# w_in loaded by contraction tile, w_out transposed on TensorE, some early loads on ScalarE's queue

## The chip, the cores and the metric

The kernel runs on one core of one Trainium2 chip. The metric is the device time of one execution in microseconds (us). The kernel before takes 674.87 us, the median of 3 runs (673.68 to 677.32).

## The reference

Three parts follow each other: a linear attention with decay over 768 steps (4 batches, 8 heads of 48), a dense layer with `g = h * cos(h)`, and a layer that sends each token to one of eight experts, or to none.

```python
# r, k, v: (4, 8, 768, 48); state starts at 0
for t in range(S):
    cur = einsum('bhd,bhe->bhde', u[None] * kt, vt)
    y[:, :, t] = einsum('bhd,bhde->bhe', rt, state + cur)
    state = w[None, :, :, None] * state + einsum('bhd,bhe->bhde', kt, vt)
x = y.transpose(0, 2, 1, 3).reshape(3072, 384)

h = x @ w_in                      # (384, 2048)
x = (h * cos(h)) @ w_out          # (2048, 384)

do_compute = x @ w_skip > 0
e_idx = argmax(x @ w_gate, axis=1)          # 8 experts
out = x                                     # where do_compute is False
out = x + gate * (relu(x @ w1[e]) @ w2[e])  # elsewhere, e of the token
```

## The kernel before

Tokens go through in 12 chunks of 256 (64 steps of each batch). For each chunk c the attention loads two tiles of r and k (`rk`, step ldr) and two of r, k, v in natural order (`nat`, step ldn), scales them on VectorE and GpSimd (km, rm, knm, pr1, pr2, cc, am), and multiplies on TensorE: A (r with k), Y (with v), Yz (with the carried state), U (the new state). The result goes into `xt` as a high and a low float16 part (xh on ScalarE, xl on VectorE), and six small transfers (xx) put 16-partition pieces in their place.

The dense layer takes the chunk as group g. G1(g, f), f = 0 to 7, multiplies `xt` by `w_in`: 18 matmuls of 256 columns into one PSUM tile, then the chain cn (ScalarE), cr (VectorE), cs (ScalarE, sine), cg (VectorE), ch (ScalarE), cl (VectorE or GpSimd) gives g in two float16 parts. G2(g, t, q), t = 0 and 1, q = 0 to 3, multiplies by w_out: 12 matmuls a quarter.

All weights are split into a high and a low part as well. The inputs w_in and w_out are 8-byte words. A piece is loaded (step ld), VectorE makes float32 of it in three passes (wu L448, wx L454, wv L460), ScalarE writes the high part (wh), VectorE or GpSimd the low one (wl). w_in comes in 8 pieces of 256 columns of all three contraction tiles, so each row gives a run of 2 KB; w_out in 8 pieces of two rows of 3 KB for each partition.

The 9 scores of the last part (skip and gate) are linear in the dense layer's output, so w_out times `w_skip` and `w_gate` gives 9 more columns of w_out (DM to NO, 384 to 393). For each of 16 tiles k of w_out two DMA transposes (wt, L508) bring its high and low part into `wt`, nine matmuls (wm) multiply it by a float16 pair of the 27 score weights (`sgh`), and at the end wph and wpl write the high and low part of all 16. The very first G2 does without these columns, and a step of its own, G2(0, 0, l), adds them later, with 48 matmuls of 9 columns.

After the twelfth group the tokens of each expert are gathered and go through the expert matmuls in 16 tiles; that part is not touched.

The order is not written by hand. Every step is added to a `Plan` with its engine, a cost, its dependences and a priority; a list scheduler in `Plan.order` sets the order on each engine from them. The table `SHIFT` moves priorities, the table `ENGINE` picks the engine of a step, and `PIECES` says in which order the pieces of w_in and w_out take their priorities. Engines then work in that order, each waiting for what its next instruction needs. The queue SP starts nearly all transfers; ScalarE (ACT) starts three at the beginning.

Of the kernel before, what the change touches and what calls it, by code (L numbers as in the profile page):

```python
# [40 lines left out]
SG = 2.0 ** 2  # L41
# [15 lines left out]
class Plan:  # L57
# [28 lines left out]
    def order(self):  # L86
# [15 lines left out]
        while any(ready.values()):  # L102
# [57 lines left out]
PIECES = "iioiiiooioioiooo"  # L160
PIECE_0, PIECE_STEP = -40, 8
SHIFT = {
# [18 lines left out]
    "sgl": 280, "tab0": 300, "tabi": -310, "tkd": -260, "tkn": -360, "tkt": 400, "vb_0_0": 50, "vb_1_1": 150,  # L181
# [13 lines left out]
):
    ENGINE.update(dict.fromkeys(_ks.split(), _e))


def group(key):
# [8 lines left out]
    if n in ("wt", "wm"):  # L208
        return f"{n}_{key[1] // 4}"
# [33 lines left out]
def _kernel(ctx, tc, rk, nat, wcol, small, ci, w_in, w_out, w1, w2, out):  # L243
# [56 lines left out]
    sgh = cp.tile([128, 2, 3, 9], F16, name="sgh")  # L300
# [43 lines left out]
    add("cst", "A", 2700, f, prio=-900, nbytes=400e3)  # L344

# [997 lines left out]
```

## Time and profile before

| | |
|---|---|
| median of 3 runs | 674.87 us |
| the profiled execution | 674.17 us |
| its span, first to last instruction | 672.4 us |
| mean granted TensorE clock | 0.961 |
| busy: TensorE, VectorE, ScalarE, GpSimd | 593.0, 423.4, 305.8, 300.8 us |
| DMA: moved, mean rate over the span | 87.04 MB, 129 GB/s |

The span is what the profile shows instruction by instruction; the execution's own time has 1.8 us more around it. PE is TensorE, PEld its weight loads, DVE VectorE, ACT ScalarE, POOL GpSimd, SP the sync engine, whose queue is SPq. TensorE's clock has two levels; the granted clock of a stretch is 1.00 if all of it ran at the upper one and 0.50 if all of it ran at the lower one. An engine's busy time in a stretch, and what ended its idle time, are read beside each other: an engine may be idle because it waits, or because it is done.

### The profile page before, as it was taken

The numbers are of one execution on the slowest core, as the hardware profiler recorded it, in microseconds if no ns is written. First come the engines' busy times: TensorE is split into PE (matmuls) and PEld (weight loads), VectorE is DVE, ScalarE is ACT, GpSimd is POOL, SyncE is SP. The second block draws the span as 40 slices with busy tenths as digits, with TensorE's granted clock in tenths as the row PEclk, the third lists the DMA queues.
The fourth block names the chain that finished last, engine by engine and source line by source line (L and its number), as shares of the span: only waits on it lengthen the run. The fifth ranks groups of instructions, "written<-read, shape, count | busy, mean of one in ns | idle before, by whom it ended". The sixth has DMA issues, their size and how long they took to land. (4 is left out here: it accounts for less than half of the span.)

```text
span 672.4 us, 17390 instructions
## 1 busy us (share of the span) xinstructions
PE 593.0 (88%) x7191; PEld 441.1 (66%) x7191; DVE 423.4 (63%) x828; ACT 305.8 (45%) x522; POOL 300.8 (45%) x269
## 2 busy tenths in 40 slices
PE   1325659699999999999999999999999989999993
PEld 1314438567768777777777777777776768777662
DVE  5877858856857654645564655454686568777650
ACT  2224536432536454444444454444674146555530
POOL 3342426456866575657464543233353152232111
PEclk9996759789999999999999999999999999999997
DMA  8979877567272215160504210010768238889820
GB/s 181 224 172 236 197 146 190 119 144 204 69 181 73 79 33 148 27 153 4 157 25 123 58 32 26 22 34 7 235 220 185 51 92 233 267 237 242 249 86 18
DMA packets 83075, 87.04 MB, mean 129 GB/s; under 512 B 35838, under 2 KB 70956, under 8 KB 82994
## 3 DMA queue, kind: packets, MB, share of 16 engines
q1 hardware_dynamic: 79746, 80.67, 47.9%
q0 software_dynamic: 2816, 4.91, 2.5%
q8 instruction: 57, 0.93, 0.6%
q10 hardware_dynamic: 432, 0.33, 0.2%
q14 instruction: 24, 0.20, 0.1%
HBM read 66.57 MB, written 13.73 MB: 119 GB/s over the span
## 5 line engine op out<-in xcount | busy, mean ns | idle before, releaser
L264 PE MATMUL ps_o<-wo,gt 128*128 128x393 f16 (+2 forms) x1200 | 211.1, 329 | 0.0
L264 PE MATMUL ps_h<-xt,wih 128*128 128x256 f16 x1152 | 200.6, 279 | 7.4 <-DVE s L741 7.4
L264 PEld LDWEIGHTS <-gt 128*128 128x128 f16 x1200 | 113.3, 99 | 76.3 <-issue 5.2
L264 PE MATMUL ps_h<-xt,wil 128*128 128x256 f16 x576 | 160.7, 279 | 0.0
L746 POOL TENSOR_TENSOR gt<-s,gt 128x512 f16<-128x512 f32 x87 | 105.1, 1214 | 107.1 <-ACT gt L274 106.7
L264 PEld LDWEIGHTS <-wih 128*128 128x128 f16 x1152 | 112.9, 100 | 29.8 <-DVE s L741 7.9
L734 DVE SCALAR_TENSOR_TENSOR s<-s,ps_h 128x512 f32<-128x512 int32 x96 | 65.4, 684 | 89.3 <-ACT s L730 89.2
L737 ACT ACTIVATE s<-s 128x512 f32<-128x512 f32 x96 | 60.0, 629 | 58.2 <-DVE s L734 58.2
L730 ACT ACTIVATE s<-ps_h 128x512 int32<-128x512 f32 x96 | 56.9, 592 | 59.4 <-PE ps_h L264 57.1
L274 ACT ACTIVATE gt<-s 128x512 f16<-128x512 f32 x87 | 54.4, 628 | 56.6 <-DVE s L741 56.6
L741 DVE SCALAR_TENSOR_TENSOR s<-s,ps_h 128x512 f32<-128x512 f32 x87 | 59.2, 683 | 33.4 <-ACT s L737 33.3
L264 PE MATMUL ps_h<-xe,w 128*128 128x256 f16 (+1 forms) x720 | 65.8, 251 | 2.9 <-issue 1.1
L264 PE MATMUL ps_o<-w,hh 128*128 128x384 f16 x384 | 64.9, 326 | 1.6 <-DVE hh L1112 1.4
L281 DVE SCALAR_TENSOR_TENSOR w<-ws,w 128x768 f16<-128x768 f32 (+1 forms) x56 | 60.0, 1084 | 8.8 <-ACT w L274 8.4
L264 PEld LDWEIGHTS <-w 128*128 128x128 f16 x720 | 58.8, 98 | 9.6 <-issue 2.3
L264 PEld LDWEIGHTS <-wil 128*128 128x128 f16 x576 | 57.8, 100 | 7.8
L274 ACT ACTIVATE w<-ws 128x768 f16<-128x768 f32 (+1 forms) x56 | 51.1, 928 | 16.8 <-DMA ws<-in_w_dram 14.0
L264 PEld LDWEIGHTS <-hh 128*128 128x128 f16 x384 | 36.9, 98 | 26.1 <-DVE hh L1112 2.5
L1141 POOL DMA_INDIRECT out_dram<-xg,recs x16 | 18.5, 1156 | 71.3 <-DVE xg L1136 54.8
L873 POOL DMA_INDIRECT tab<-rec,di x24 | 24.6, 1025 | 45.6 <-DVE osum L867 23.1
L552 POOL TENSOR_TENSOR k<-rk,tk 112x512 f32<-112x512 f32 x20 | 27.7, 1383 | 33.9 <-DMA rk<-in_rk_dram 26.3
L1107 ACT ACTIVATE hh<-ps_h 128x512 f16<-128x512 f32 (+1 forms) x40 | 20.2, 510 | 35.7 <-PE ps_h L264 31.4
(129 smaller groups left out, 614.8 us busy)
## 6 DMA issues: line engine op xcount, KB each, us to landing
nat<-in_nat_dram SPq DMA_DIRECT2D x96, 144.0 KB, 4.5
ws<-in_w_dram SPq DMA_DIRECT2D x24, 512.0 KB, 5.6
ws<-in_w_dram SPq DMA_DIRECT2D x32, 384.0 KB, 4.5
rk<-in_rk_dram SPq DMA_DIRECT2D x24, 448.0 KB, 5.5
so<-in_w_out_dram SPq DMA_DIRECT2D x8, 768.0 KB, 11.3
xd<-y SPq DMA_DIRECT2D x24, 192.0 KB, 2.0
out_dram<-y SPq DMA_DIRECT2D x48, 96.0 KB, 2.2
si<-in_w_in_dram SPq DMA_DIRECT2D x16, 192.0 KB, 5.8
```

The costliest lines, as they stand in the source:

```text
L264: return T.matmul(o, lhsT=l, rhs=r, start=start, stop=stop)
L274: return A.activation(out=o, in_=i, func=AF.Copy, scale=scale)
L281: V.scalar_tensor_tensor(out=o, in0=x, scalar=scale, in1=hi, op0=ALU.mult, op1=ALU.subtract)
L552: add((name, c, x), e, cost, lambda: ENG[e].tensor_tensor(out=o(), in0=a(), in1=b(), op=op), deps, pr)
L730: A.activation(out=n, in_=d["ph"], func=AF.Copy, scale=1.0 / (TWO_PI * SH), bias=0.25)
L734: V.scalar_tensor_tensor(out=d["s"], in0=d.pop("n"), scalar=-TWO_PI * SH, in1=d["ph"], op0=ALU.mult, op1=ALU.add)
L737: lambda: A.activation(out=d["s"], in_=d["s"], func=AF.Sin, scale=1.0 / SH, bias=math.pi / 2), [("cr", g, f)], pr)
L741: V.scalar_tensor_tensor(out=o, in0=s, scalar=0.5, in1=ph, op0=ALU.mult, op1=ALU.mult)
L746: lambda: ENG[e].tensor_tensor(out=gt[g][1][:, 2 * f:2 * f + 2], in0=d.pop("g"), in1=gt[g][0][:, 2 * f:2 * f + 2], op=ALU.subtract), [("ch ...
L873: P.indirect_dma_start(out=tab[:, :], out_offset=bass.IndirectOffsetOnAxis(ap=di[:, t], axis=0), in_=rec[:, t], in_offset=None, bounds_che ...
L1107: A.activation(out=d["hh"][:, 0, 2 * f_:2 * f_ + 2, 0:N], in_=d["ph", f_][:, :, 0:N], func=AF.Relu)
L1141: P.indirect_dma_start(out=out[:, :], out_offset=bass.IndirectOffsetOnAxis(ap=xo["recs"][:, s, 1:2], axis=0), in_=xs_.pop(s), in_offset=No ...
```

## The change

- **w_in** comes in 6 pieces instead of 8: one contraction tile of 128 rows and half of the columns each, so a row gives a run of 8 KB. A piece takes four transfers, to 48 and 16 partitions at a time. G1(g, f) now needs three pieces: all three contraction tiles of its half.
- **w_out** is transposed on TensorE: six matmuls with an identity add the high and the low part into PSUM (wt), ScalarE copies the float32 result (wc), three float32 matmuls multiply it by the scores' weights (wm), and ScalarE and VectorE write the high and low part of these 9 columns for each k (wph, wpl). The two PSUM tiles of G2 serve for it in turn. The first group's G2 has the 9 columns from the start, waits for all 16 wpl, and the step G2(0, 0, l) is gone.
- **Queues:** a load whose step stands in the new table row "A" of `ENGINE` is started by ScalarE.
- The tables `SHIFT`, `ENGINE` and `PIECES` have other numbers, so the order on every engine is another.

```diff
-PIECES = "iioiiiooioioiooo"
+PIECES = "ioiiioiioooooo"
...
+    ("A", """ld_i_0 ld_i_4 ld_o_0 ld_o_6 ld_o_7 ldn_0_1 ldn_1_0 ldn_3_0 ldn_3_1 ldr_2_1 ldr_3_1 xx_2"""),
...
+    def dq(eng):
+        return A if eng == "A" else nc.sync
...
-    def w_in_piece(f_, prio):
-        def src(t):
-            m = slice(256 * WW * f_, 256 * WW * (f_ + 1))
-            v = w_inv[0:288, m].rearrange("(j i p) n -> i p j n", j=3, i=2)
-            x = w_inv[288:384, m].rearrange("(i j p) n -> i p j n", i=2, j=3)
-            for i in range(2):
-                nc.sync.dma_start(out=t[64 * i:64 * i + 48, 0:3:2], in_=v[i, :, 0:3:2])
-                nc.sync.dma_start(out=t[64 * i:64 * i + 48, 1], in_=v[1 - i, :, 1])
-                nc.sync.dma_start(out=t[64 * i + 48:64 * i + 64], in_=x[1 - i])
+    def w_in_piece(i, prio):
+        j, m = i % 3, slice(F_ * (i // 3), F_ * (i // 3 + 1))
+        def src(t, q):
+            for x in range(2):
+                a, b = 96 * j + 48 * (x ^ (j % 2)), 288 + 48 * (1 - x) + 16 * j
+                v = w_inv[:, WW * m.start:WW * m.stop].unsqueeze(1)
+                q.dma_start(out=t[64 * x:64 * x + 48], in_=v[a:a + 48])
+                q.dma_start(out=t[64 * x + 48:64 * x + 64], in_=v[b:b + 16])
...
-            wt_[k] = wt = ap.tile([128, 2, 3, 128], F16, tag="wt", name="wt", bufs=2)
-            for i in range(2):
-                nc.sync.dma_start_transpose(out=wt[:, i], in_=wo[:, k, i, 0:DM])
-        add(("wt", k), "Q", 2400, f, [("wl", "o", k // 2), ("wm", k - 2)], wpr["o", k // 2] - 50, 100e3)
+            wt_["p", k] = p = pt("o", [128, 512], bufs=2)
+            for j in range(3):
+                for i in range(2):
+                    mm(p[:, 128 * j:128 * j + 128], wo[:, k, i, 128 * j:128 * j + 128], ident, i == 0, i == 1)
+        add(("wt", k), "PE", 330, f, [("wl", "o", k // 2), "cst16", ("wpl", k - 2)], wpr["o", k // 2] - 5)
...
+            wt_["t", k] = t = ap.tile([128, 3, 128], F32, tag="wt", name="wt", bufs=2)
+            copy(A, t.rearrange("p a b -> p (a b)"), wt_["p", k][:, 0:DM])
+        add(("wc", k), "A", c_a(DM, True), f, [("wt", k), ("wm", k - 2)], wpr["o", k // 2] - 5)
...
             for j in range(3):
-                mm(p, wt[:, 0, j], sgh[:, 0, j], j == 0, False)
-                mm(p, wt[:, 0, j], sgh[:, 1, j], False, False)
-                mm(p, wt[:, 1, j], sgh[:, 0, j], False, j == 2)
+                mm(wt_["p", k][:, DM:NO], t[:, j], wsgs[:, j], j == 0, j == 2)
...
-            [("xx", g), ("xl", g, 0), ("xl", g, 1), ("wl", "i", f), pv("cg", 3), pv("cl", 3) if pv("cl", 3) in pl.steps and pl.steps[pv("cl", 3)][0] == "V" else None] + free, pr)
+            [("xx", g), ("xl", g, 0), ("xl", g, 1), *(("wl", "i", 3 * (f // 4) + j) for j in range(3)), pv("cg", 3), pv("cl", 3) if pv("cl", 3) in pl.steps and pl.steps[pv("cl", 3)][0] == "V" else None] + free, pr)
...
-            deps += [("wl", "o", k) for k in range(2 * q, 2 * q + 2)] + [("wm", 0) if alone else "wpl"]
+            deps += [("wpl", k) for k in range(KF)] if i < 2 else []
-        if alone:
-            add(last, "PE", 1200, lambda: part(range(KF), slice(DM, NO)), [("G2", g, t, 3), "wpl"], pr + 50)
```

What it makes of the order on the engines, at three places. The start of SP's queue before, from the first instruction on (wc and us are small constants, rk and nat the loads of chunk 0, si a piece of w_in):

```order
L332 DMA wc<-in_wcol_dram 112x4
L337 DMA us<-in_small_dram 64x2x48 x4
L556 DMA rk<-in_rk_dram 112x1024 x2
L576 DMA nat<-in_nat_dram 64x3x192 x8
L481 DMA si<-in_w_in_dram 48x2x512
L482 DMA si<-in_w_in_dram 48x512
L483 DMA si<-in_w_in_dram 16x3x512
```

And now:

```order
L337 DMA wc<-in_wcol_dram 112x4
L342 DMA us<-in_small_dram 64x2x48 x4
L570 DMA rk<-in_rk_dram 112x1024 x2
L592 DMA nat<-in_nat_dram 64x3x192 x4
L493 DMA si<-in_w_in_dram 48x2048
L494 DMA si<-in_w_in_dram 16x2048
```

Half of the chunk's nat transfers have gone to ScalarE's queue, and w_in moves up.

ScalarE between the first and the second nat copy of chunk 1 (vf), ahead of its first cn, before (wo and wih are high parts of weights, cv the float32 of a piece):

```order
L274 ACTIVATE vf_87<-nat 128x8x48
L274 ACTIVATE wo<-cv 128x2x384
L274 ACTIVATE cv<-cv 128x768
L274 ACTIVATE wih<-cv 128x3x256 x2
L274 ACTIVATE vf_88<-nat 128x8x48
```

And now, from the same copy on (wt is the copy wc, wo<-ps_o the step wph):

```order
L279 ACTIVATE vf_87<-nat 128x8x48
L279 ACTIVATE wt<-ps_o 128x384 x2
L279 ACTIVATE wo<-ps_o 128x9 x2
L493 DMA si<-in_w_in_dram 48x2048
L494 DMA si<-in_w_in_dram 16x2048
```

The first two tiles of w_out are copied there, and a piece of w_in is started behind them (two more such transfers, one of rk and then vf_88 follow).

VectorE around the low part of the 9 score columns before (s is the activation chain, cc a reduction of the attention):

```order
L552 TENSOR_TENSOR pr<-nat 128x384
L734 SCALAR_TENSOR_TENSOR s<-s,ps_h 128x512
L741 SCALAR_TENSOR_TENSOR s<-s,ps_h 128x512
L281 SCALAR_TENSOR_TENSOR wo<-ps_o,wo 128x16x9
L585 TENSOR_REDUCE cc<-pr 128x8
```

And now around the last but one of them:

```order
L752 SCALAR_TENSOR_TENSOR s<-s,ps_h 128x512
L601 TENSOR_REDUCE cc<-pr 128x8
L564 TENSOR_TENSOR k_1314<-rk,tk 112x512
L286 SCALAR_TENSOR_TENSOR wo<-ps_o,wo 128x9
L759 SCALAR_TENSOR_TENSOR s<-s,ps_h 128x512
```

One subtraction for all 16 tiles has become 16 small ones, spread over the opening; the last follows one row further down. On TensorE all 16 G1 of the first two groups, and wt and wm of all 16 tiles, now stand ahead of the first G2; before, four quarters of G2(0, 0) stood between them.

## Rows read from the trace of the kernel before

**Rows 1.** Busy time of the engines by stretches, granted clock, DMA; the first line names columns.

```profile
core 0: us, PE busy (x) PEld busy (x) DVE busy (x) ACT busy (x) POOL busy (x), PEclk, DMA share, GB/s
0.00:139.30 139.30, 74.99 (x1060) 57.36 (x1060) 104.54 (x149) 54.56 (x94) 57.53 (x49) 0.85 0.82 179
139.30:672.40 533.10, 518.02 (x6135) 383.69 (x6131) 318.82 (x679) 251.20 (x428) 243.28 (x220) 0.99 0.43 116
...
47.20:139.50 92.30, 64.91 (x820) 48.77 (x816) 71.63 (x95) 42.39 (x70) 40.69 (x32) 0.78 0.77 168
...
140.00:150.00 10.00, 10.00 (x121) 5.98 (x111) 5.81 (x11) 3.23 (x7) 6.06 (x5) 0.83 0.77 188
```

**Rows 2.** TensorE's waits, 0 to 160 us: us in total, times, longest.

```profile
PE ps_o L264 <- DMA wt<-wo: 17.7, 12, 5.2
PE ps_ay L264 <- POOL k L552: 12.6, 1, 12.6
```

**Rows 3.** VectorE's waits, 0 to 140 us: us in total, times, longest.

```profile
DVE cv L448 <- DMA si<-in_w_in_dram: 14.3, 5, 7.2
DVE wo L281 <- ACT wo L274: 4.8, 2, 3.0
DVE s L734 <- ACT s L730: 4.7, 4, 2.1
DVE pr L552 <- POOL pr L552: 2.9, 1, 2.9
DVE cv L448 <- DMA so<-in_w_out_dram: 2.7, 2, 2.3
```

**Rows 4.** SP's queue in order of time: start us, us, what it starts.

```profile
26.20 5.36 SPq L576 DMA_DIRECT2D nat<-in_nat_dram  x4
...
116.66 10.37 SPq L508 DMA_TRANSPOSE wt<-wo  x8
```

**Rows 5.** The tile wt: ns of one start, min/median/max, first and last us.

```profile
L508 SPq DMA_TRANSPOSE wt<-wo x32: 1177/1206/1349, 46.2 to 135.2; - x32
```

**Rows 6.** VectorE: groups of 0 to 140 us, then single rows in order of time.

```profile
L734 DVE SCALAR_TENSOR_TENSOR s<-s,ps_h 128x512 f32<-128x512 int32 x16 | 10.9, 680 | 4.7 <-ACT s L730 4.7
L552 DVE TENSOR_TENSOR k<-rk,tk 112x512 f32<-112x512 f32 x3 | 2.1, 689 | 0.8 <-DMA rk<-in_rk_dram 0.8
...
27.01 0.95 DVE L281 SCALAR_TENSOR_TENSOR wil<-cv,wih 128x768 f16<-128x768 f32 x1
...
45.60 5.87 DVE L281 SCALAR_TENSOR_TENSOR wil<-cv,wih 128x768 f16<-128x768 f32 x1
...
144.41 0.16 DVE L787 TENSOR_SCALAR lg<-ps_o 128x9 f32<-128x9 f32 x1
```

**Rows 7.** TensorE in order of time: start us, us, instruction and count.

```profile
47.27 0.61 PE L264 MATMUL ps_h<-xt,wih 128*128 128x256 f16 x2
...
129.91 2.11 PE L264 MATMUL ps_o<-wo,gt 128*128 128x384 f16 x12
...
139.32 1.11 PE L264 MATMUL ps_ay<-r,zs 48*48 48x64 f32 x64
140.37 19.15 PE L264 MATMUL ps_o<-wo,gt 128*128 128x9 f16 x144
```

**Rows 8.** TensorE groups: 9-column float16, float32 transposes; busy us, mean ns | idle before.

```profile
L264 PE MATMUL ps_o<-sgh,wt 128*128 128x9 f16 x144 | 7.1, 170 | 17.9 <-DMA wt<-wo 17.7
...
L1047 PE MATMUL ps_ay<-cfs,xg 128*128 128x128 f32 x6 | 1.0, 272 | 0.0
```

**Rows 9.** Stretches as in rows 1; the last: packets, MB, share, 500 to 506 us.

```profile
0.00:10.00 10.00, 1.01 (x4) 0.66 (x4) 6.18 (x19) 3.50 (x12) 1.61 (x6) 1.00 0.65 154
14.00:34.00 20.00, 6.01 (x160) 5.28 (x160) 16.83 (x24) 4.03 (x6) 7.68 (x6) 1.00 1.06 224
500.00:506.00 6.00, 6.00 (x48) 4.47 (x46) 4.69 (x7) 5.15 (x9) 2.67 (x3) 1.00 0.96 334
...
q1 hardware_dynamic: 1088, 1.60, 76.3%
```

More of the change, by code (lines that the diff above doesn't have):

```diff
@@ L40 @@
 SO = SH * SWO / 2
-SG = 2.0 ** 2
 SX2 = 2.0 ** 6
@@ L119, in order @@
             if nbytes:
-                n = max(1, min(3, int(cost // 450)))
+                n = max(1, min(6, int(cost // 450)))
                 over = at + cost
@@ L207, in group @@
         return f"ld_{key[1]}{key[2]}"
-    if n in ("wt", "wm"):
+    if n in ("wt", "wc", "wm", "wph", "wpl"):
         return f"{n}_{key[1] // 4}"
@@ L400, in f @@
         copy(A, ones, cst("ones"))
-        copy(A, sgh[:, 0], wsgs, SG)
+        copy(A, ident, cst("ident"))
     add("cst16", "A", 600, f, ["cst"], -100)
-    add("sgl", "V", 100, lambda: lo(sgh[:, 1], wsgs, sgh[:, 0], SG), ["cst16"], -100)
     def f():
@@ L433, in f @@
                 t_[0] = mp.tile(shape, WT, tag=f"g{(i + 1) % 2}", name="si", bufs=2)
-            src_fn(t_[0])
+            src_fn(t_[0], dq(eq))
         back = 2 if kind == "o" else 4 if i < 4 else 2
-        add(("ld",) + key, "Q", 450 if kind == "o" else 1800, f, [("wv", kind, i - back)], prio - 150,
+        eq, cost = on(("ld",) + key, "Q", **{x: 450 if kind == "o" else 1800 for x in "QA"})
+        add(("ld",) + key, eq, cost, f, [("wv", kind, i - back)], prio - 150,
             4 * 128 * shape[1] * shape[2])
@@ L554, in att, with f @@
         for h in range(2):
-            def f(h=h):
-                nc.sync.dma_start(out=tile_(("rk", h), [112, 2, HB, C], 1, f"ld_rk{h}"), in_=rk[2 * c + h])
-            add(("ldr", c, h), "Q", 450, f, [("rm", c - 1, h), ("km", c - 1, h)], pp + 20 * h - 100, 459e3)
+            eq, cost = on(("ldr", c, h), "Q", Q=450, A=450)
+            def f(h=h, eq=eq):
+                dq(eq).dma_start(out=tile_(("rk", h), [112, 2, HB, C], 1, f"ld_rk{h}"), in_=rk[2 * c + h])
+            add(("ldr", c, h), eq, cost, f, [("rm", c - 1, h), ("km", c - 1, h)], pp + 20 * h - 100, 459e3)
             def bt(t, h=h):
@@ L569, in att, with f @@
             d["vf", j], d["kf", j] = vfs[i], kfs[i]
-            def f(j=j):
+            eq, cost = on(("ldn", c, j), "Q", Q=1800, A=1800)
+            def f(j=j, eq=eq):
                 t = tile_(("nat", j), [128, 3, HB, D], 1, f"ld_nat{j}")
@@ L575, in f @@
                     for p in range(2):
-                        nc.sync.dma_start(out=t[R2[p], :, B * h:B * h + B], in_=v[p])
-            add(("ldn", c, j), "Q", 1800, f, [(x, c - 1, j) for x in ("knm", "vb", "pr1")], pj - 95, 590e3)
+                        dq(eq).dma_start(out=t[R2[p], :, B * h:B * h + B], in_=v[p])
+            add(("ldn", c, j), eq, cost, f, [(x, c - 1, j) for x in ("knm", "vb", "pr1")], pj - 95, 590e3)
             ld = ("ldn", c, j)
@@ L666, in att, with f @@
             add(("xl", c, p), "V", c_v(nk), f, [("xh", c, p)], by)
-        def f():
+        eq, cost = on(("xx", c), "Q", Q=2700, A=2700)
+        def f(eq=eq):
             for j in range(3):
                 for i in (48, 112):
-                    nc.sync.dma_start(out=xt[c][i:i + 16, j], in_=xt[c][i - 48 + 16 * j:i - 32 + 16 * j, 3])
-        add(("xx", c), "Q", 3600, f, [("xl", c, 0), ("xl", c, 1)], by - 50, 100e3)
+                    dq(eq).dma_start(out=xt[c][i:i + 16, j], in_=xt[c][i - 48 + 16 * j:i - 32 + 16 * j, 3])
+        add(("xx", c), eq, cost, f, [("xl", c, 0), ("xl", c, 1)], by - 50, 100e3)
         for p in range(2) if c < NC - 1 else ():
@@ L721, in fn @@
                     mm(ph[:, q], wil[:, j, m], x[:, j, 0], False, j == 2)
[L722 removed]
+        free = [("G2", g - 2, t, q) for t in range(2) for q in (3,)] if g > 1 else [("wv", "i", 2 * g + j) for j in (2, 3)]
         add(("G1", g, f), "PE", 1970, fn,
[L724 removed]
+            [("xx", g), ("xl", g, 0), ("xl", g, 1), *(("wl", "i", 3 * (f // 4) + j) for j in range(3)), pv("cg", 3), pv("cl", 3) if pv("cl", 3) in pl.steps and pl.steps[pv("cl", 3)][0] == "V" else None] + free, pr)
         def fn():
@@ L757, in prev @@
             return (name, j // 2, j % 2) if j >= 0 else None
-        alone = i == 0
-        last = ("G2", g, t, "l" if alone else 3)
-        def part(ks, cols):
-            gh, gl = gt[g]
-            m = slice(128 * t, 128 * t + 128)
-            p = d["p"][:, cols]
-            for k in ks:
-                mm(p, gh[:, k, m], woh[:, k, cols], k == 0, False)
-                mm(p, gh[:, k, m], wol[:, k, cols], False, False)
-                mm(p, gl[:, k, m], woh[:, k, cols], False, k == KF - 1)
+        last = ("G2", g, t, 3)
         for q in range(4):
@@ L775, in fn @@
                     d["p"] = po[i] = pt("o", [128, 512], bufs=2)
-                part(range(4 * q, 4 * q + 4), slice(0, DM if alone else NO))
+                gh, gl = gt[g]
+                m = slice(128 * t, 128 * t + 128)
+                p = d["p"][:, 0:NO]
+                for k in range(4 * q, 4 * q + 4):
+                    mm(p, gh[:, k, m], woh[:, k], k == 0, False)
+                    mm(p, gh[:, k, m], wol[:, k], False, False)
+                    mm(p, gl[:, k, m], woh[:, k], False, k == KF - 1)
             deps = [("cl", g, 2 * q), ("cl", g, 2 * q + 1), ("G2", g, t, q - 1), prev("yo", 2), prev("lg", 2), ("rb", g - 1) if t and g else None,
                     "clv" if t and g == GE + 1 else None]
-            deps += [("wl", "o", k) for k in range(2 * q, 2 * q + 2)] + [("wm", 0) if alone else "wpl"]
+            deps += [("wpl", k) for k in range(KF)] if i < 2 else []
             add(("G2", g, t, q), "PE", 2015, fn, deps, pr + 10 * q + 15)
-        if alone:
-            add(last, "PE", 1200, lambda: part(range(KF), slice(DM, NO)), [("G2", g, t, 3), "wpl"], pr + 50)
         def fn():
```

34 lines of the change are left out of this document (17 added, 17 removed), and 53 rows, old and new, of the table SHIFT.

## The prediction

> **What bounds the kernel now.** I read the granted clock and the span first (one core, 672.4 us), then the busy time of the engines by stretches [rows 1]. TensorE is the bound from 139.3 us on: of the 533.1 us behind that point it is busy 518.0, and its own waits there lie in the expert stage and the tail, which the change hardly touches. Ahead of that point it is busy 75.0 of 139.3 us, part of it at the lower clock of 1.2 GHz, half of 2.4 (the stretch from 47.2 to 139.5 was granted 0.78). So the change can win only in the opening, and the question is one number: **T**, the moment from which TensorE is fed without a gap. Before, T = 139.3.
>
> Who TensorE waits for in the opening comes next [rows 2]: 17.7 us in 12 pieces for the DMA-transposed w_out (wt), 12.6 for a product of the attention. But a wait removed there is worth only what the next one leaves. The second product reads all of w_out, and what makes w_out ready is VectorE: it is busy 104.5 of the 139.3 us [rows 1], and its 34.8 idle us are 17.0 for loads (14.3 + 2.7), 9.5 for ScalarE (4.8 + 4.7), 2.9 for GpSimd [rows 3]; the 5.4 left are the first constants and small pieces. The sync queue shows the transposes from its side: starting one takes 1.2 us [rows 5], eight took 10.37 us, and loads stand behind them; a queue that is full charges plain transfers too, 5.36 us for four [rows 4].
>
> **The change part by part.**
> *w_out's transposes.* 32 starts of 1.2 us leave the sync queue, 38.6 us in all, and their packets leave the DMA engines. In their place each of 16 k gets, on TensorE, six 128-column matmuls (wt) and three float32 ones with 9 columns (wm), a ScalarE copy of 384 columns (wc), a ScalarE copy (wph) and a VectorE subtraction of 9 columns (wpl). TensorE: 12 matmuls of 384 columns take 2.1 us from start to end, some 0.167 each [rows 7], so 128 columns are 0.056 and 96 of them 5.3 us. The float32 ones have no row: the 9-column f16 matmuls they replace took 7.1/144 = 0.05, six float32 transposes 1.0 us, 0.17 each [rows 8]; I take the upper one, since both are float32 with a full 128x128 operand: 48 x 0.17 = 8.2 (2.4 at the other end). Against the 7.1 removed that is +6.4 us, in the opening, beside VectorE's work.
>
> *G2 of the first group* no longer has its 9 extra columns done apart: 48 matmuls go. They were the first third of 144 that took 19.15 us [rows 7]; the other 96 at 0.167 are 16.0, so 3.1 us.
>
> *The order on TensorE.* In the changed program both groups' G1 (16 of them) and all wt and wm stand ahead of the first G2, and that G2 waits for every wpl. So T is now the last wpl (plus a G1 that overlaps it), and four G2 quarters that before were done ahead of T come behind it: 4 x 2.0 = 8.0, and one attention product of 64 matmuls, 1.1 [rows 7]. What is left behind T: 533.1 + 8.0 + 1.1 - 3.1 - 1.7 (the 10 us from 140 were granted 0.83, so 3.4 us at half clock, which give back half) [rows 1] = **537.4**. The span is T + 537.4, if nothing behind T starts to wait.
>
> *VectorE up to the last wpl,* counted in the two orders of instructions. The conversions are the same elements in 14 pieces for 16: 0. More: eight attention products taken from GpSimd at 0.69 [rows 6], 5.5; two subtractions of the activation chain, 1.4; 16 wpl at the 0.16 of the nearest row, a 9-column read of PSUM, [rows 6], less the single one it replaces, 2.3. Less: three steps of the activation chain at 0.68, two masked copies and a reduction of the third attention chunk, now later, 4.0. Sum +5.2. One row comes off: a subtraction that is 0.95 elsewhere took 5.87 [rows 6] while GpSimd was at its own products, and in the new order most of those are VectorE's; I take 4.9 off (0 to 4.9). So 104.5 + 5.2 - 4.9 = **104.8** (to 109.7).
>
> *VectorE's idle time.* I keep the start and the small pieces (5.4) and the waits for ScalarE (9.5), which gets 32 short copies more. GpSimd's 2.9 goes, since VectorE does that product itself. Of the 17.0 for loads I keep 4: ahead of and with the first w_in piece the queues carry 5.3 MB (chunk 0, constants, one w_out piece, two w_in pieces), at the 224 GB/s of that stretch [rows 9] 23.7 us, and VectorE is through its work ahead of it at about 19. Later loads are 2 to 8 us early by the same count, for no transpose stands ahead of them. Idle 18.9, between 5.4 (only the start) and 34.8 (nothing gained).
>
> *Sum.* **T = 104.8 + 18.9 = 123.7, span 123.7 + 537.4 = 661.1.** The profiled execution took 674.17 us with a span of 672.4, so 1.8 lies around it: 662.9, taken as **663.0**, 1.7% under that execution. The median of the runs, 674.87, is 0.7 above the profiled one.
>
> *Loads on ScalarE's queue:* 35 starts move there. ScalarE is busy 54.6 of the 139.3 us [rows 1], and unloaded starts cost it little; the dear case is a rival. *Three w_in pieces ahead of the first G1* instead of one: TensorE starts G1 some us later than before, which costs nothing while VectorE sets T.
>
> *Size of the runs.* In the stretch of 2 KB rows of w_in (and 768-byte ones) the engines are full at 224 GB/s; around 500 us they move 334 with 1.60 MB in 1088 packets, 1.5 KB each [rows 9]. So small packets alone don't hold the early loads down. The Trainium skill, DMA: Bandwidth & Descriptors, Specifications, says that 512 bytes are enough for line rate; the rows agree, and by it 8 KB runs would gain nothing, which is the second rival; my sum uses 224 and no gain.
>
> **The rivals.**
> 1. *The starting waits alone remain.* Two queues bring everything ahead of need and ScalarE keeps up: idle near 5.4, T = 110, time 649. For it: DMA stood at 0.65 in the first 10 us [rows 9]. Against: engines that wait for each other in order seldom close up like this. 0.15.
> 2. *w_in comes no faster, and it comes in a lump:* w_in still goes to 48 and 16 partitions at a time, and three whole pieces are wanted ahead of the first G1. Then 11 of the 17.0 us stay: T = 130.7, time 669.9. For: the 224 GB/s above. Against: the loads that were late stood behind transposes. 0.13.
> 3. *The round trip takes the place of the transposes.* wt, wc, wm, wph, wpl cross TensorE, ScalarE and VectorE, two PSUM buffers allow two k at a time, and G1 stands behind them on TensorE. G1 starts no earlier than its 47.3 before [rows 7]; TensorE's work up to T is 16 x 2.0 for G1 (its 18 x 256 columns equal 12 x 384), 13.5 for wt and wm, some 5 of attention: 50.5, at the 0.78 of that stretch 65, so T would be 112 without waits. Eight pairs of k with hand-overs of 1.2 us each (4.7 in 4, [rows 3]), two or three a pair, add 22: T = 134, time 673, no change. For: G1 gives little cover when wm follows its wt at once. Against: other work stands between most of them. 0.12.
> 4. *Slower: ScalarE blocks while it starts transfers.* Before its first sine it starts 18 more, 13 of them when the queues are full, and three later among w_out's copies; at some 1.2 us each (5.36 for four, [rows 4], was 1.3) that is 19 us in which its copies, which VectorE needs, stand still. If VectorE waits for all of it, T = 123.7 + 19 = 142.7, time 681.9. It loses from 12 us on (T above 135). Against: ScalarE is idle more than half of that time. 0.10.
>
> **How the numbers follow.** Forecast 0.50 (T between 115 and 128: 654 to 668); rivals 0.15, 0.13, 0.12, 0.10. A measurement of this kernel tells a change from none at about 0.5%, 3.4 us. Faster by more: the forecast, rivals 1 and 2 nearly whole, a little of 3: 0.77. Within: 0.13. Slower: 0.10. The range runs from rival 1 to just past rival 3: 648 to 676.
>
> **What would show it.** Right: no wait for wt's DMA, TensorE without a gap from about 124 us, VectorE busy near 85% up to there with under 6 us for loads, the last 9-column subtraction just ahead of the first G2. Wrong: ScalarE idle behind its own DMA starts (rival 4); TensorE waiting for ScalarE's wt copies in many pieces (3); VectorE waiting for si (2). The rest behind T would be wrong if TensorE waited there, most likely where the third group's G1 follows the six small xt transfers that ScalarE now starts; I give that 0 to 3 us.

## The result: slower by 1.1%

The changed kernel takes 681.84 us, the median of 6 runs (680.12 to 684.77), beside 674.66 for the kernel before on the same chip. The ratio is 1.0114, 95% interval 1.0086 to 1.0142. The prediction was 663.0 with a range of 648 to 676, so both the time and the sign were wrong. The profiled execution of the changed kernel took 684.77 us with a span of 683.0; it was the slowest of the six, 2.9 us above their median. Of the runs further down, the time of the first experiment leaves out one execution of ten, 688.67 us, which fell in a slower state.

By the sum's own terms the span has come out 21.9 us above the 661.1 that I worked out: T, the moment from which TensorE is fed without a gap, is 140.2 for 123.7 (16.5 us), and what lies behind T is 542.8 for 537.4 (5.4 us). Beside the kernel before, T is 0.9 us later and the rest 9.7 us longer: the gain ahead of T did not come, and the price behind it was higher than the 4.3 of the sum.

### The profile page after: what moved, and what is told of

Read it like the earlier page. It is cut to its first block, busy times and chain, and to the rows that moved or that the text cites. A ratio compares the mean times of both kernels' runs of the same rounds, so it can differ in the third digit from the quotient of the medians.

```text
span 683.0 us, 17347 instructions
## 1 busy us (share of the span) xinstructions
PE 601.2 (88%) x7191; PEld 451.4 (66%) x7191; DVE 427.3 (63%) x848; ACT 312.0 (46%) x550; POOL 286.1 (42%) x255
## 5 line engine op out<-in xcount | busy, mean ns | idle before, releaser
L269 PE MATMUL ps_o<-wo,gt 128*128 128x393 f16 x1152 | 204.3, 330 | 0.0
L269 PEld LDWEIGHTS <-gt 128*128 128x128 f16 x1152 | 110.8, 98 | 73.2
L764 POOL TENSOR_TENSOR gt<-s,gt 128x512 f16<-128x512 f32 x85 | 101.6, 1200 | 116.7 <-ACT gt L279 112.5
L759 DVE SCALAR_TENSOR_TENSOR s<-s,ps_h 128x512 f32<-128x512 f32 x85 | 57.8, 681 | 26.3 <-ACT s L755 26.2
L1151 POOL DMA_INDIRECT out_dram<-xg,recs x16 | 20.0, 1250 | 61.9 <-DVE xg L1146 50.7
L564 POOL TENSOR_TENSOR k<-rk,tk 112x512 f32<-112x512 f32 x19 | 25.0, 1318 | 31.8 <-DMA rk<-in_rk_dram 21.6
## 6 DMA issues: line engine op xcount, KB each, us to landing
si<-in_w_in_dram SPq DMA_DIRECT2D x8, 384.0 KB, 14.3
```

The costliest lines, as they stand in the source:

```text
L269: return T.matmul(o, lhsT=l, rhs=r, start=start, stop=stop)
L564: add((name, c, x), e, cost, lambda: ENG[e].tensor_tensor(out=o(), in0=a(), in1=b(), op=op), deps, pr)
L759: V.scalar_tensor_tensor(out=o, in0=s, scalar=0.5, in1=ph, op0=ALU.mult, op1=ALU.mult)
L764: lambda: ENG[e].tensor_tensor(out=gt[g][1][:, 2 * f:2 * f + 2], in0=d.pop("g"), in1=gt[g][0][:, 2 * f:2 * f + 2], op=ALU.subtract), [("ch ...
L1151: P.indirect_dma_start(out=out[:, :], out_offset=bass.IndirectOffsetOnAxis(ap=xo["recs"][:, s, 1:2], axis=0), in_=xs_.pop(s), in_offset=No ...
```

## The profile after

Stretches of the changed kernel, with the columns of [rows 1]: up to T, behind T, and the stretch from 14 to 44 us, in which the early loads run.

```profile
0.00:140.20 140.20, 75.76 (x996) 64.21 (x997) 101.85 (x164) 60.26 (x120) 39.75 (x33) 0.94 0.72 157
140.20:683.00 542.80, 525.40 (x6197) 387.14 (x6195) 325.47 (x685) 251.75 (x430) 246.37 (x223) 0.99 0.41 114
...
14.00:44.00 30.00, 6.25 (x169) 5.66 (x170) 19.34 (x26) 5.81 (x8) 3.57 (x3) 1.00 1.06 162
```

TensorE is still the bound behind T. Ahead of T it is busy 75.8 us, VectorE 101.9: three us under my 104.8. But VectorE is idle 38.3 us there, not 18.9. And the DMA engines, full in the stretch of the early loads (share 1.06), move 162 GB/s there, where the prediction took 224 from [rows 9].

VectorE's waits, 0 to 140 us (us in total, times, longest), as in [rows 3]:

```profile
DVE cv L458 <- DMA si<-in_w_in_dram: 9.1, 1, 9.1
DVE r L564 <- DMA rk<-in_rk_dram: 7.8, 3, 3.4
DVE wo L286 <- ACT wo L279: 4.0, 4, 2.0
...
DVE pr L564 <- DMA nat<-in_nat_dram: 2.8, 1, 2.8
...
DVE kf L564 <- DMA nat<-in_nat_dram: 2.1, 2, 1.3
...
DVE cv L458 <- DMA so<-in_w_out_dram: 1.5, 1, 1.5
```

The waits for loads add up to 9.1 + 7.8 + 2.8 + 2.1 + 1.5 = 23.3 us; I had kept 4. What the first one does is seen in VectorE's own order of time (start us, us, instruction, idle before it):

```profile
23.46 0.69 DVE L564 TENSOR_TENSOR am<-cfs,cc 128x512 f32<-128x512 f32 x1
33.26 0.69 DVE L458 TENSOR_SCALAR cv<-si 128x1024 int32<-128x1024 int32 x1 [9.10 <-DMA si<-in_w_in_dram]
33.86 0.72 DVE L627 COPY_PREDICATED am<-cis,ps_ay 128x512 f32<-128x512 int32 x1
```

The conversion of the first w_in piece waits 9.1 us for its load. The masked copy behind it had its operands (with quicker loads it runs at 24.99 us without a wait, as is shown further down), but it has to wait for its turn in VectorE's order. TensorE waits for that copy, as its waits from 0 to 160 us show, with the columns of [rows 2]:

```profile
PE ps_ay L269 <- DVE am L627: 17.7, 1, 17.7
PE ps_ay L269 <- POOL k L564: 13.8, 2, 11.3
...
PE ps_o L269 <- ACT wt L279: 5.8, 6, 1.9
```

The wait for the DMA transposes, 17.7 us in [rows 2], is gone, and one of the same size for a masked copy of the attention has come. The round trip of rival 3 cost 5.8 us in six pieces. TensorE's order of time shows both ends of its opening:

```profile
65.45 0.61 PE L269 MATMUL ps_h<-xt,wih 128*128 128x256 f16 x2 [1.30 <-DMA xt<-xt]
...
140.23 18.26 PE L269 MATMUL ps_o<-wo,gt 128*128 128x393 f16 x108
```

The first G1 came 18.2 us later than the 47.3 of [rows 7], and from there to the first G2 without a gap it was 74.8 us instead of 92.0. So the change shortened the second part of the opening by 17 us, and the first part lost as much.

The new work on TensorE, 0 to 145 us (busy us, mean ns, idle before it):

```profile
L269 PE MATMUL ps_o<-wsgs,wt 128*128 128x9 f32 x96 | 13.8, 273 | 5.8 <-ACT wt L279 5.8
L269 PE MATMUL ps_o<-ident,wo 128*128 128x128 f16 x96 | 8.8, 248 | 2.3 <-DVE wo L286 1.6 <-POOL wo L482 0.7
```

48 float32 matmuls leave 96 records, two each, and take 0.29 us apiece. Together 22.6 us, where the prediction had 13.5.

## The experiments

Theory A: w_in's transfers to 48 and 16 partitions load slowly, and the change depends on them more. Rivals: ScalarE stands still while it starts transfers (B); three whole pieces are wanted ahead of the first G1 (C); the transposes on TensorE cost (D). Each ratio below is to the kernel before.

### Shorter runs, one queue, the old pieces

In the first kernel each w_in transfer was cut in two that can't be joined, in runs of 2 KB:

```diff
-                q.dma_start(out=t[64 * x:64 * x + 48], in_=v[a:a + 48])
-                q.dma_start(out=t[64 * x + 48:64 * x + 64], in_=v[b:b + 16])
+                o = t.rearrange("p o (c r n) -> p (o c) r n", c=2, r=2)
+                w = v.rearrange("p o (c r n) -> p (o c) r n", c=2, r=2)
+                for r in range(2):
+                    q.dma_start(out=o[64 * x:64 * x + 48, :, r], in_=w[a:a + 48, :, r])
+                    q.dma_start(out=o[64 * x + 48:64 * x + 64, :, r], in_=w[b:b + 16, :, r])
```

> The changed kernel, with each w_in transfer cut into runs of 2 KB (8 transfers a piece for 4); order and queues as in the changed kernel. Theory A, long runs to 48 and 16 partitions are slow: the packets of w_in go from some 10 GB/s an engine to some 12, 3 MB of w_in take 13 to 16 us for 19, VectorE's single wait for si (9.1 us) falls under 6, the first G1 comes at 58 to 62 us for 65.4, and the time falls to 674 to 679. Theory C, three whole pieces are wanted ahead of the first G1 and the length of the run is nothing: first G1 at 65, time 681 to 684. Against both: 24 more starts of 0.6 to 1.3 us in the opening can take 5 us back, which would show as longer waits on the queues of SP and ScalarE.

Measured: 680.38 us, ratio 1.0073 (1.0047 to 1.0100), not separable from the change. The first G1 came at 61.6 us and the first G2 at 132.8, 7.4 us earlier, but the span was only 3.5 shorter. VectorE waited 7.3 us for nat where it had waited for si. For T, 132.8, the length of the run is worth 7.4 of the 16.5 us; for the time it is a small part, since 546.7 us now lie behind T for 542.8.

In the second all starts went back to SP (`return nc.sync` in `dq`), in the planned order.

> The changed kernel, with all loads started by SP, in the order that was planned. Theory B, ScalarE blocks while it starts transfers (8.0 us at ldn of chunk 1, 3.9 at chunk 0): its waits leave, first G1 5 to 10 us earlier, time 672 to 677. Theory A or C, the loads themselves are late: SP's queue gets some 30 us more of starts ahead of the first G1, and the time is 682 to 692.

Measured: 678.78 us, ratio 1.0046 (1.0018 to 1.0074). So starts on ScalarE cost some 0.7%, about 4.6 us; B is a part of the loss. The first G1 came at 55.6 us, 9.8 earlier, and T at 131.1, 9.1 earlier, with w_in's transfers in the same form; behind T lay 550.0. VectorE's waits for loads added up to 19.8 us for 23.3, so SP's longer list of starts did not make them later.

In the third w_in had its old eight pieces (the lines of w_in and `PIECES` of the diff undone).

> The changed kernel, with w_in in 8 pieces of 256 columns as before (runs of 2 KB, one piece wanted for the first G1); transposes on TensorE and loads on ScalarE's queue stay, the priorities are those of the change. Theories A and C: the first G1 comes back to 47 to 53 us, the way from there to the first G2 stays near 75 us as in the changed kernel, so that the first G2 starts near 122 to 130 and the time is 661 to 672. If the transposes on TensorE are what costs (theory D): first G1 early, but the first G2 still near 140, time 679 to 684.

Measured: 708.38 us, ratio 1.0506 (1.0473 to 1.0539), which none of the theories had. The first G1 came at 56.6 us, but the last transposes came at 165 us and the first G2 at 168.4. I put that down to the priorities of the change, which were chosen for other pieces. It says nothing about the loads.

### The loads by themselves

```python
def phase(load):          # one form after the other, into the same tile
    load(t)
    V.tensor_copy(out=s, in_=...)      # waits for all of it
```

> No computation of the reference: it only loads the same 3.1 MB nine times over, one form after the other, each waiting for the one ahead to land. In order: (1) w_in as in the change, 12 transfers of 48 and 16 partitions by 8 KB; (2) w_in as before, 24 transfers, runs of 2 KB; (3) as 1 but in runs of 2 KB; (4) 3 transfers of 128 partitions by 8 KB; (5) 4 transfers of 128 partitions by three runs of 2 KB; (6) w_out, 4 transfers of 128 partitions by two runs of 3 KB; (7) as 1, started by SP and ScalarE in turn; (8) as 1 and (9) as 2 again. Theory A (long runs are slow): 1 and 4 take 18 to 21 us, 2, 3 and 5 13 to 16. If 48 and 16 partitions are what is slow, and not the length: 1, 2 and 3 alike at 16 to 20 us, 4, 5 and 6 at 10 to 14. If neither (the other loads beside it made it slow in the kernel): all within 2 us of each other, apart from the starts.

VectorE's idle time ahead of each read is the time of a form. Forms 2 to 9 in order (form 1 ran beside the writing of the output and is left out):

```profile
60.19 0.15 DVE L61 COPY s<-t 128x1 int32<-128x1 int32 x1 [21.52 <-DMA t<-in_w_in_dram]
...
78.57 0.15 DVE L61 COPY s<-t 128x1 int32<-128x1 int32 x1 [17.84 <-DMA t<-in_w_in_dram]
...
89.59 0.15 DVE L61 COPY s<-t 128x1 int32<-128x1 int32 x1 [10.48 <-DMA t<-in_w_in_dram]
...
101.51 0.15 DVE L61 COPY s<-t 128x1 int32<-128x1 int32 x1 [11.41 <-DMA t<-in_w_in_dram]
...
112.44 0.15 DVE L61 COPY s<-t 128x1 int32<-128x1 int32 x1 [10.41 <-DMA t<-in_w_out_dram]
...
132.25 0.15 DVE L61 COPY s<-t 128x1 int32<-128x1 int32 x1 [19.30 <-DMA t<-in_w_in_dram]
...
155.54 0.15 DVE L61 COPY s<-t 128x1 int32<-128x1 int32 x1 [22.75 <-DMA t<-in_w_in_dram]
...
176.32 0.15 DVE L61 COPY s<-t 128x1 int32<-128x1 int32 x1 [20.24 <-DMA t<-in_w_in_dram]
```

3.15 MB to 48 and 16 partitions take 22.75 us in the form of the change (138 GB/s) and 20.2 to 21.5 in the form before; to 128 partitions 10.48 us with runs of 8 KB (300 GB/s) and 11.41 with 2 KB (276). The partitions of a transfer are worth a factor of two, the length of the run 9% at 128 partitions, and at 48 and 16 the long run is the slower one.

> No computation of the reference: the same 3.1 MB in rows of 8 KB, loaded with 128, 96, 64, 48, 32, 16 and again 128 partitions a transfer (3, 4, 6, 8, 12, 24 and 3 transfers), each form after the one ahead has landed. If the rate goes by the partitions of a transfer: 10.5 us for 128, some 12 to 14 for 96, 15 to 21 for 64 and 48, above 20 for 32 and 16. If the uneven pair of 48 and 16 is what is slow: 64 and 32 take 10 to 13 as well. If it is the starts (0.3 to 0.4 us each): 128 to 48 within 3 us, 16 near 20.

The form here is read by one to four instructions; the idle times of one form add up. 96, 64 (two), 48 (two), 32 (four), 16 and 128 partitions; the first line is the output, which SP started to write just ahead of the form of 96:

```profile
10.48 0.35 SPq L71 DMA_DIRECT2D out_dram<-z  x1
36.28 0.36 DVE L65 TENSOR_REDUCE s<-t 96x1 int32<-96x128 int32 x1 [24.96 <-DMA t<-in_w_in_dram]
51.64 0.30 DVE L65 TENSOR_REDUCE s<-t 64x1 int32<-64x96 int32 x1 [14.99 <-DMA t<-in_w_in_dram]
53.95 0.31 DVE L65 TENSOR_REDUCE s<-t 64x1 int32<-64x96 int32 x1 [2.00 <-DMA t<-in_w_in_dram]
72.97 0.36 DVE L65 TENSOR_REDUCE s<-t 48x1 int32<-48x128 int32 x1 [18.71 <-DMA t<-in_w_in_dram]
75.03 0.36 DVE L65 TENSOR_REDUCE s<-t 48x1 int32<-48x128 int32 x1 [1.71 <-DMA t<-in_w_in_dram]
88.61 0.30 DVE L65 TENSOR_REDUCE s<-t 32x1 int32<-32x96 int32 x1 [13.21 <-DMA t<-in_w_in_dram]
...
119.02 0.31 DVE L61 TENSOR_REDUCE s<-t 128x1 int32<-128x96 int32 x1 [26.62 <-DMA t<-in_w_in_dram]
129.43 0.31 DVE L65 TENSOR_REDUCE s<-t 128x1 int32<-128x96 int32 x1 [10.09 <-DMA t<-in_w_in_dram]
```

The three later readings of 32, left out here, add 3.5 us. With the short readings between the waits: 128 partitions 10.1 us, 32 16.7, 64 17.3, 48 20.8, 16 26.6. The 25.0 us of 96 are no price of that form: the output's 4608 KB were written beside it, from the start at 10.48 us to their landing 13.5 us later, and with them gone the page shows 249 GB/s from 26 to 33 us. By that, 96 partitions lie between 128 and 64; alone they were not measured. The output's KB and us to landing, and the rate of the 40 slices of 3.26 us:

```profile
out_dram<-z SPq DMA_DIRECT2D x1, 4608.0 KB, 13.5
...
GB/s 116 409 422 379 362 362 364 294 249 249 171 88 226 208 231 201 38 186 166 178 171 168 68 146 226 211 216 166 95 136 131 121 121 126 128 108 28 344 429 166
```

The uneven pair is not the cause, since 64 and 48 partitions alone are slow too. Neither are the starts: twelve transfers of 32 take no longer than six of 64. And the DMA engines were busier with the slow form of the run ahead (share 0.90) than with the quick one (0.79), so they did not stand waiting for starts. What is slow is 64 partitions and fewer.

The Trainium skill, SBUF — State Buffer, section "Door 1: The DMA port swizzle", says that a transfer's rate goes by the ports that its partitions reach, that 64 partitions reach no more of them than 32, and that 128 reach all. The rows agree on 128, 64 and 32 (312, 182 and 188 GB/s). The rule of 512 bytes that the prediction cited from the Trainium skill (DMA: Bandwidth & Descriptors, Specifications) agrees with the rows at 128 partitions, where runs of 2 KB and 8 KB are near each other (276 and 300 GB/s); it says nothing about fewer partitions.

### Rows of w_in in the order of the partitions

w_in's rows were laid out in memory as the partitions want them, so that a piece is one transfer of 128 partitions. The rows are put in that order with the other inputs, ahead of the execution, so the measured time doesn't hold the reordering:

```diff
-            for x in range(2):
-                ...
-                q.dma_start(out=t[64 * x:64 * x + 48], in_=v[a:a + 48])
-                q.dma_start(out=t[64 * x + 48:64 * x + 64], in_=v[b:b + 16])
+            q.dma_start(out=t, in_=v[128 * j:128 * j + 128])
```

> The changed kernel, with the rows of w_in laid out in memory in the order of the partitions, so that a piece is one transfer of 128 partitions by 8 KB in place of four of 48 and 16; order of all other instructions and queues as in the changed kernel. Theory A (revised by the loads alone: 138 GB/s for 48 and 16 partitions, 300 for 128): the 3.1 MB of the first three pieces cost some 10 us less, VectorE's wait for si falls from 9.1 to under 4, the first G1 comes at 50 to 58 us for 65.4, the first G2 at 125 to 133, time 668 to 677. Rival (what is won ahead of the first G2 is given back behind it, as half of it was with runs of 2 KB: first G2 7.4 us earlier, span 3.5 less): first G2 at 128 to 133, time 677 to 681.

Measured: 669.42 us, ratio 0.9952 (0.9928 to 0.9975), 1.6% under the change with every other instruction in the same place. Its stretches:

```profile
0.00:120.60 120.60, 74.17 (x997) 63.85 (x997) 101.04 (x160) 58.41 (x118) 38.81 (x32) 0.94 0.61 179
120.60:667.50 546.90, 525.82 (x6197) 387.01 (x6194) 327.51 (x689) 253.03 (x432) 245.16 (x223) 0.99 0.42 114
14.00:44.00 30.00, 9.54 (x184) 8.59 (x184) 24.40 (x35) 7.52 (x13) 6.01 (x4) 1.00 0.88 276
```

And VectorE at the place that is shown above of the change:

```profile
23.78 0.69 DVE L561 TENSOR_TENSOR am<-cfs,cc 128x512 f32<-128x512 f32 x1
24.39 0.69 DVE L458 TENSOR_SCALAR cv<-si 128x1024 int32<-128x1024 int32 x1
24.99 0.72 DVE L624 COPY_PREDICATED am<-cis,ps_ay 128x512 f32<-128x512 int32 x1
```

The 9.1 us are gone, the first G1 comes at 50.1, T is 120.6, earlier than was expected. VectorE is busy 101.0 and idle 19.6 us up to T, near the 104.8 and 18.9 of the prediction; its waits for loads are 7.5 us, all for nat and rk. w_in also takes 6 starts for 24 here, but in the change the DMA engines were full (1.06) while they moved 162 GB/s, and here they move 276 at 0.88, so it is the transfers that got quicker. Theory A is shown. Against the change T fell by 19.6 us and the span by 15.5; the rest is given back behind T, where 546.9 us lie for 542.8.

> As the run ahead, and all loads started by SP. If slow w_in loads and ScalarE's standing at its starts are two causes, their gains add (4 to 5 us from the starts): time 664 to 672. If both remove the same wait of VectorE and TensorE, the time is that of the run ahead, within 2 us. If SP alone can't start it all in time: 3 to 8 us above it.

Measured: 665.79 us, ratio 0.9894 (0.9853 to 0.9936). The gain over the run ahead has the size of the one without the new layout, but the two intervals touch. T came at 116.8: the layout alone took 19.6 us off T and the starts alone 9.1, both together 23.4, so in part they remove the same waits.

> The kernel before, with the rows of w_in laid out in the order of the partitions and each piece one transfer of 128 partitions by three runs of 2 KB in place of six of 48 and 16; nothing else. Theory A: VectorE's 14.3 us for si fall under 6, the first G1 comes some 5 us earlier, and SP has 40 starts fewer; time 664 to 671. Rival: VectorE waits for what stands behind, or the DMA transposes set the first G2 all the same; time 672 to 677.

Measured: **655.61 us, ratio 0.9758 (0.9724 to 0.9793)**, the fastest of all, and more than was expected. The kernel before had the same slow loads: from 14 to 34 us the full DMA engines now move 330 GB/s, for 224 in [rows 9]. Its stretches up to T and behind:

```profile
0.00:123.30 123.30, 72.90 (x1060) 56.09 (x1060) 108.48 (x149) 54.53 (x94) 60.77 (x49) 0.90 0.82 205
123.30:652.80 529.50, 515.77 (x6131) 383.08 (x6131) 320.19 (x680) 251.57 (x428) 243.96 (x220) 0.99 0.44 117
```

VectorE's waits for si are gone and it is busy 88% of the time up to T = 123.3. TensorE's wait for the DMA transposes fell from 17.7 to 9.1 us with no transpose changed, so half of it came from the w_in loads, or from their 40 starts fewer on the queue that also starts the transposes; this run doesn't tell these two apart.

### The parts alone

The kernel before with only the transposes of the change (the lines of wt, wc, wm, wph, wpl and of G2's dependences in the diff):

> The kernel before, with w_out transposed by TensorE as in the change; w_in's pieces, queues and priorities as before, the order planned anew from them. If the transposes on TensorE are a gain by themselves: no wait for wt's transfers (17.7 us before), first G1 near 47, first gapless G2 at 122 to 132, time 662 to 670. If they cost (round trip over ScalarE and VectorE, and VectorE's 16 short instructions): TensorE's waits for ScalarE's copies of wt above 10 us, time 676 to 690.

Measured: 679.10 us, ratio 1.0104 (1.0070 to 1.0139). TensorE waited for ScalarE's copies of wt only 2.9 us, so the cost is not that hand-over. T came at 135.4, 3.9 us earlier than in the kernel before, but 539.5 us lay behind it for 533.1. VectorE's waits for si fell from 14.3 to 7.4 us with the transposes off SP's queue and the order planned anew. With w_in's rows in order added:

> The kernel before with two parts: rows of w_in in the order of the partitions (one transfer of 128 partitions a piece, by itself 655.6 us) and w_out transposed by TensorE as in the change (by itself 679.1). If the transposes on TensorE cost by themselves (TensorE's 13 to 15 us of wt and wm, four quarters of G2 that move behind the last of them): 656 to 664. If they cost only because VectorE and ScalarE were held up by late loads: 646 to 654.

Measured: 668.36 us, ratio 0.9882 (0.9821 to 0.9942), 1.2% above the same kernel with DMA transposes. The cost stays when the loads are quick. The stretches say where it is:

```profile
0.00:122.60 122.60, 78.20 (x1124) 65.90 (x1125) 112.62 (x171) 64.63 (x130) 67.10 (x53) 0.90 0.69 194
122.60:666.20 543.60, 525.10 (x6067) 386.11 (x6066) 313.66 (x673) 248.87 (x424) 236.69 (x217) 0.99 0.40 111
```

T is 122.6 beside 123.3: with quick loads, taking away TensorE's 9.1 us of waits for the transposes hardly moves it. VectorE is busy 92% of the time up to there, so I read it as what sets T in this run; that was not tried apart. Behind T lie 14.1 us more. 9.3 of them are TensorE's own work (525.10 less 515.77), of which the prediction's count gives 8.0 to the four G2 quarters that with DMA transposes are done ahead of T, in TensorE's idle time, and now wait for the last wpl. The other 4.8 are idle time and the end. The moved quarters are the cost by this count; a first G2 without the nine columns, with the transposes on TensorE, was not tried. Nor was another order: the priorities here are those of the kernel before, chosen for DMA transposes.

Whether TensorE's price for the narrow matmuls matters was tried apart. The copy wc and the score weights in float16, in this kernel and in the one with SP's starts:

```diff
-            wt_["t", k] = t = ap.tile([128, 3, 128], F32, tag="wt", name="wt", bufs=2)
+            wt_["t", k] = t = ap.tile([128, 3, 128], F16, tag="wt", name="wt", bufs=2)
...
-                mm(wt_["p", k][:, DM:NO], t[:, j], wsgs[:, j], j == 0, j == 2)
+                mm(wt_["p", k][:, DM:NO], t[:, j], sgh[:, j], j == 0, j == 2)
```

> The kernel before with rows of w_in in order and w_out transposed by TensorE (668.4 us), and now the transposed copy and the score weights in float16 with 9 columns in place of float32 (their low halves are left out, so the scores are rounded). In the run without this, the float32 matmuls of 9 columns are busy 13.9 us on TensorE, the transposes 7.8. If TensorE's own work for the scores is what the transposes cost: busy falls by some 10 us and the time to 657 to 662. If the cost is in the hand-overs to ScalarE and VectorE or in the four quarters of G2 that wait for all 16: 665 to 668.

```profile
L263 PE MATMUL ps_o<-sgh,wt 128*128 128x9 f16 x48 | 3.2, 171 | 2.1 <-ACT wt L273 1.7
```

Measured: 667.40 us, ratio 0.9860 (0.9804 to 0.9915). 13.9 us of float32 matmuls became 3.2, TensorE was busy 8.6 us less in all, and the span stayed at 666.2: the waits grew by as much.

> The changed kernel with rows of w_in in order and all starts on SP (665.8 us), with the same float16 scores (low halves left out). If TensorE's own work for the scores is on the path: 655 to 660, level with the kernel before with rows in order (655.6). If not: 663 to 666, and what is left of the distance lies in the order of the change.

Measured: 667.11 us, ratio 0.9874 (0.9806 to 0.9942), the same as without: T came 2.5 us earlier, at 114.3, and 549.8 us lay behind it for 548.6. The price of the float32 matmuls, which I had taken too low, is not on the path. The six transposing matmuls for each k were not tried.

The kernel before with only the new pieces of w_in, loaded slowly and then with rows in order:

> The kernel before, with w_in in the six pieces of the change (one contraction tile and half of the columns, four transfers of 48 and 16 partitions by 8 KB, three pieces wanted for the first G1); transposes by DMA and all starts on SP as before, the order planned anew from the priorities of before. Theory: the first G1 waits for 3.1 MB at some 140 GB/s in place of one piece of 0.8 MB and comes 8 to 15 us later than 47.3; time 678 to 692. Rival: the DMA transposes set the first G2 whatever the first G1 does, 672 to 678.

> The kernel before with w_in in the six pieces of the change, but its rows in the order of the partitions, so that a piece is one transfer of 128 partitions by 8 KB. Beside the 655.6 us of eight pieces by columns with rows in order it shows what three pieces ahead of the first G1 cost when the loads are quick: 3 pieces of 1 MB at 300 GB/s take 10.5 us against 2.6 for one, and three pieces of conversion by VectorE some 11 against 4. Theory (order of the pieces matters): 660 to 670. Rival (only the partitions matter): 654 to 658.

Measured: 688.35 us, ratio 1.0185 (1.0121 to 1.0249), and 672.24, ratio 0.9946 (0.9917 to 0.9974). The second is above both of its forecasts. With slow loads the first G1 came at 62.9 us, with quick ones at 45.5; in both the new pieces cost 1.9% beside the old ones. With them comes a wait that the change doesn't have, here of the slow one (25.0 us in the quick one):

```profile
PE ps_o L264 <- DMA wt<-wo: 41.7, 14, 23.9
```

w_out's pieces come after nearly all of w_in in the new `PIECES`, so the DMA transposes come late. In company of the transposes on TensorE the pieces by tile (665.8 to 669.4) and by columns (668.4) come out level, in other orders of work though: what C costs by itself was not told apart.

## Why the prediction was wrong, point by point

- **The bound: right, "one number" not.** Behind T TensorE is fed, 525.4 of 542.8 us. But what lies behind T moved by 9.7 us and T by 0.9.
- **VectorE's work up to T: right.** 101.9 us for 104.8.
- **"Of the 17.0 for loads I keep 4": this step failed.** It was 23.3, and VectorE's idle time 38.3 for 18.9: of the 19.4 us more, 19.3 are waits for loads. With 2.9 us less of work that makes the 16.5 us by which T was late. The step took 224 GB/s from a stretch of [rows 9] in which other loads ran among those of w_in. In the change three whole pieces of w_in, all in transfers of 48 and 16 partitions, stand ahead of the first G1; the stretch went at 162 GB/s, and alone such transfers go at 138. *Size of the runs* asked the wrong question: length is worth little in time, as it said, but the partitions of a transfer were not priced. The same row held the hint: the engines were full at 224 GB/s and elsewhere moved 334 in packets that were no longer. I read that as "not the packets' size" and stopped. With quick loads in the same order T is 120.6, 3.1 us ahead of the sum. Quick loads are not the only thing that brings T forward, though: with 48 and 16 partitions kept, shorter runs gave 7.4 us of it and starts on SP 9.1.
- **"No transpose stands ahead of them": half of it.** The step expected the later loads early because the transposes leave SP's queue, and held against rival 2 that the late loads stood behind transposes. Without them, and with the old loads, VectorE's waits for si were 7.4 us for 14.3; with them, and quick loads, there were none.
- **A late load holds up more than its user.** One conversion stood 9.1 us in VectorE's order ahead of a masked copy that was ready, and TensorE waited 17.7 us for that copy (8.9 with quick loads).
- **Rival 2 came nearest:** w_in did come "no faster"; whether the lump cost by itself was not told apart. The 11 us of waits that it kept were half of the 23.3.
- **Rival 3:** TensorE's waits in the round trip were 5.8 us, not 22. **Rival 4:** ScalarE's starts cost about 4.6 us of time and 9.1 of T, not 19; it stood 8 us at four of them, most of which VectorE spent waiting for w_in.
- **The transposes' price on TensorE:** 22.6 us for 13.5, mis-sized. Taking 10.7 us off it did not change the time.
- **"Four quarters that come behind T":** right in kind, too low in size. Behind T it was 542.8 for 537.4. 3.1 of these 5.4 us are TensorE's work (525.4 for 518.0 + 4.3): the 48 matmuls of 9 columns that left took 1.4 us and not 3.1, since the row of [rows 7] that I divided by three joined them with 96 of 393 columns. Most of the other 1.7 is the lower clock of those 96 (granted 0.50 from 142 to 145 us), which the sum took off a second time. 2.3 are idle time.
- **The term behind T fails by itself too.** With T at 120.6 there lay 546.9 us behind it, 9.5 above the 537.4; so with the loads put right the time was 669.42, still 6.5 above the 662.9. Beside the 533.1 of before that is 13.8 us more for the 4.3 of the sum: 7.8 of TensorE's work and 6.0 of idle time. In the runs with the transposes on TensorE this rest was 535.0 (third experiment, with T at 168.4) to 550.0 us, in the two with DMA transposes and the old pieces 533.1 and 529.5.
- **What sets T was read as VectorE alone.** In the kernel before its last conversion of w_out ends at 120.6 us. The last four transposes are started between 131 and 137 us, and TensorE waits for them until 139.06, just ahead of T. So there the transposes stood at the end of the opening. Taking them to TensorE moved T by 3.9 us with slow loads and by 0.7 with quick ones. From SP's and TensorE's order of time in the kernel before:

```profile
131.39 5.20 SPq L508 DMA_TRANSPOSE wt<-wo  x4
...
138.60 0.21 PE L264 MATMUL ps_o<-sgh,wt 128*128 128x9 f16 x2 [1.35 <-DMA wt<-wo]
139.06 0.33 PE L264 MATMUL ps_o<-sgh,wt 128*128 128x9 f16 x7 [0.25 <-DMA wt<-wo]
```

## What to carry to other kernels

Before changing the length or the queue of a load, price its form: bytes over the time from start to landing, against another load of the same kernel at full share. Here a transfer to 48 and 16 partitions went at half the rate of one to 128, and laying out the rows ahead of the execution so that one transfer spans all 128 was worth 2.4%, where three other edits lost 1.1%. In an experiment on loads, look at what else moves: a form that ran beside the output's write looked twice as slow as it was. Work that the bound engine does while it waits for another is free, and an edit that removes its wait but moves such work behind the wait can lose.

## What the runs showed of the hardware

- The same 3.15 MB went at 312, 182, 151, 188 and 118 GB/s to 128, 64, 48, 32 and 16 partitions a transfer, each form once. 48 is slower than 32, which I can't explain from these runs.
- At 48 and 16 partitions two queues were faster than one, each form once: 19.30 us with SP and ScalarE in turn, 22.75 with SP alone.
- Starting a transfer took 0.31 to 0.43 us where nothing held it up. In the changed kernel SP stood 10.40 us at two loads of rk and ScalarE 8.04 us at four of nat, behind the pieces of w_in:

```profile
47.69 10.40 SPq L570 DMA_DIRECT2D rk<-in_rk_dram  x2
...
24.69 8.04 ACTq L592 DMA_DIRECT2D nat<-in_nat_dram  x4
```

- A float32 matmul of 9 columns took 0.29 us on TensorE (13.8 us for 48) and a float16 one 0.07 (3.2 us for 48), in the same place in the order.
